# Decode attention, two layers on one core: the scores of heads 2 to 12 move from matmuls to VectorE multiply-and-sums, with their keys laid out by key

## The chip, the core and the metric

The kernel runs on one core of a Trainium2 chip. A core has a matrix engine (TensorE, "PE" in the profile), a vector engine (VectorE, "DVE"), a scalar engine (ScalarE, "ACT"), GpSimd ("POOL") and a queue engine (SyncE, "SP") that here issues nearly all transfers between the chip's memory (HBM) and on-chip memory (SBUF). Matmul results land in a small accumulator memory (PSUM). The metric is the device time of one execution, in microseconds; three timed runs of the kernel before took 1323.81 to 1325.99 us, with a median of 1324.0.

## The reference

The input `x` is two rows (batch 2, one token each) of 448 numbers. Two layers are applied, each an attention over a cache and then a gated feed-forward block, with a layer norm ahead of each and the result added back to `x`. Both layers use the same caches and weights.

```
q = (layernorm(x) @ wq)              # 16 heads of 256
scores = q . k_cache * 256**-0.5     # per head and row: 4096 keys of 256
p = softmax(scores)
o = p . v_cache
x = x + o @ wo
gate = layernorm(x) @ W_gate;  up = layernorm(x) @ W_up     # 448 -> 1792
x = x + (gate * (gate > 0) * up) @ W_down
```

All in float32. One head of one batch row has 4 MB of keys and 4 MB of values, so a layer reads 268 MB of cache, and what the second layer can't find on the chip it reads again.

## The kernel before

**Units.** The work of a layer is cut into 32 units, one for each pair of head and batch row, `u = 0..31`. The first layer takes heads 0 to 15, the second heads 15 to 0, so that the last keys and values of the first layer can stay on the chip (22 chunks of 1 MB, `KEPT`).

**Staging.** SBUF holds an arena of 27 slots of 1 MB: six blocks of four slots and three single ones. Keys and values come as whole 4 MB blocks in one transfer, except near the start of the second layer and the ends of both (`grouped`), where they come by 1 MB. The weights of a head (`wq` and `wo` parts, "h", 896 KB) go to a single slot and leave its last 256 columns free. Feed-forward weights come through the same slots. `pump` issues transfers on SP in one fixed order, as soon as the order of releases in the program frees a slot or a block; each transfer then waits on the chip for the last reader of that place. A unit's order of loads is keys, the next head's weights (every second unit), values.

**A unit.** `query(u)`, once for a head, makes the query of both rows as a column (256 numbers over 128 partitions, two halves) and pads it into `q_pad`. `score(u, c)` is run for four 1 MB chunks: the host has laid the keys out so that a chunk has 128 of a key's 256 numbers down the partitions, and four matmuls of 128x512 per chunk give the scores in PSUM (`rawa` or `rawb`) spread over a few partitions. `score_copy` brings them to `found_s` (VectorE), and `score_turn` turns them by four small matmuls into 128 partitions x 32 columns. `softmax_max` takes the maximum (VectorE, then GpSimd over the partitions), `softmax_exp` the exponentials and their sum (ScalarE, GpSimd). `weigh(u, c)` multiplies them with the values, 16 matmuls of 128x512 a unit into `poa` or `pob`. `softmax_sum`, `out_copy` and `out_add` scale and add the two halves into `row`; `out_turn` and `out_keep` turn that row into a column, and `project` (every second unit) multiplies it with `wo` and adds to `y` in PSUM.

**What sets the order.** The order is written out by hand (`manual_schedule`), and each engine runs its own instructions in that order; semaphores between engines are put in automatically. `scores(u)` interleaves the end of unit `u - 1` (`out_turn`, `out_keep`, `project`) between the chunks of unit `u`; `outputs(u)` follows.

**Layer start.** `absorb` makes the centred input `xT` from `y`. `again` writes the residual back into `y` by two matmuls, so that `project` can add to it. `busy(n, half)` issues n dummy matmuls, whose results nobody reads, between steps in which PE waits.

Of the kernel before, what the change touches and what calls it, by code (L numbers as in the profile page):

```python
# [9 lines left out]
AF = mybir.ActivationFunctionType  # L10
ALU = mybir.AluOpType
# [3 lines left out]
B, D, H, S, DH, F = 2, 448, 16, 4096, 256, 1792  # L15
P = 128
DC = 5
FULL, TAIL = 3, 64
NT = S // P
CT = 8  # L20
UNIT = CT * DH
# [6 lines left out]
SMALL = 13  # L28
ENDS = 4
AHEAD = 4  # L30
EPS = 1e-5
SCALE = DH**-0.5

# [32 lines left out]
def two_layers(  # L66
# [10 lines left out]
    nc = tc.nc  # L77
# [10 lines left out]
    arena = consts.tile([P, (BLOCKS * NC + SINGLES) * UNIT], F32, name="arena")  # L88
# [6 lines left out]
    at_of = {}  # L95
# [16 lines left out]
    def pump():  # L112
        while pending:
            at = None
            for i, ((kind, name, c), n) in enumerate(pending[: AHEAD if pending[0][1] == 1 else 1]):
                if i and kind != "h":
# [20 lines left out]
    def get(*key):  # L137
        at = at_of[key]
        return arena[:, at * UNIT : (at + 1) * UNIT]
# [45 lines left out]
    row = consts.tile([P, 2 * DH], F32, name="row")  # L185
    found_s = consts.tile([P, 2 * DH], F32, name="found_s")
# [23 lines left out]
    eps_t = consts.tile([P, 1], F32, name="eps_t")  # L210
    nc.vector.memset(eps_t, EPS)

# [5 lines left out]
    xT = xr[:, :, :, 0]  # L218
# [3 lines left out]
    raw = [ps_r.tile([P, 2 * DH], F32, name=f"raw{k}") for k in "ab"]  # L222
# [14 lines left out]
    def busy(n, half):  # L237

        for _ in range(n):
            nc.tensor.matmul(  # L240
                po_all[half][:B, :DH], ident[:, :B],
                ident[:, None, :].to_broadcast([P, 2, P]), start=True, stop=True,
            )
# [23 lines left out]
    def again():  # L267

        for half in range(2):
            n = D - DH if half else DH  # L270
            nc.tensor.matmul(
                y[32 * half : 32 * half + B, :n], halves[:, half], yrow[:, :n],
                start=True, stop=False,
            )

    def squares():
        sq = work.tile([P, FULL + 1, B], F32, name="sq")
        nc.vector.tensor_mul(sq, xT[:, : FULL + 1], xT[:, : FULL + 1])
        total = work.tile([P, B], F32, name="total")
        nc.vector.reduce_sum(total, sq.rearrange("p c b -> p b c"), axis=AX.X)  # L280
        return total
# [9 lines left out]
    def attention(order, after):  # L291
# [4 lines left out]
        q_of, oT_of, s_of, mx_of, p_of, r_of, po_of, pT_of = ({} for _ in range(8))  # L296
# [3 lines left out]
        def query(u):  # L300
            h = order[u][0]
            w = get("h", h, 0)
            pq = pq_all
            for j in range(2):
                if j and u == 0:
                    again()
                for c in range(FULL):
                    at = c * DH + j * P
                    nc.tensor.matmul(  # L309
                        pq[:, j, :], w[:, at : at + P], xT[:, c, :], start=(c == 0), stop=False  # L310
                    )
                nc.tensor.matmul(  # L312
                    pq[:, j, :], w[:, FULL * DH : FULL * DH + P], xT[:, FULL + j, :],
                    start=False, stop=True,
                )
            q = q_pad[:, u // 2 % 2]
            nc.vector.tensor_copy(q[..., 1], pq)
            for v in (u, u + 1):
                q_of[v] = q[:, :, order[v][1]]

        def spread(total):

            deviation(total)
            nc.scalar.activation(nsr[:, :1], eps_t, AF.Exp)
            inverse()
            nc.vector.tensor_scalar_mul(sr, rstd, SCALE)
            nc.vector.tensor_scalar_mul(nsr, rstd, -SCALE)
# [42 lines left out]
        def softmax_sum(u):  # L370
            ri = work.tile([P, 1], F32, name="ri")
            nc.vector.reciprocal(ri, r_of[u])
            r_of[u] = work.tile([P, 2], F32, name="ri2")
            nc.vector.tensor_scalar_mul(r_of[u], lead, ri)

        def weigh(u, c):


            vt = get("v", order[u], c)
            if c == 0:  # L380
                po_of[u] = po_all[u % 2]
            for t in range(CT if u == n_u - 1 else 0):
                n = c * CT + t
                nc.tensor.matmul(
                    po_of[u][32 * (t % 4) : 32 * (t % 4) + 1, :DH],
                    p_of[u][:, n : n + 1],
                    vt[:, t * DH : (t + 1) * DH],
                    start=(c == 0 and t < 4),
                    stop=(c == NC - 1 and t >= 4),
                )  # L390
            for t in range(CT // 2 if u < n_u - 1 else 0):
                n = c * CT + 2 * t
                nc.tensor.matmul(  # L393
                    po_of[u][32 * t : 32 * t + 2, :],
                    p_of[u][:, n : n + 2],
                    vt[:, 2 * t * DH : (2 * t + 2) * DH],
                    start=(c == 0),
                    stop=(c == NC - 1),
                )
            if ("v", order[u], c) not in after:  # L400
                release("v", order[u], c)

        def out_copy(u):
            nc.scalar.activation(row[:, :DH], po_of[u][:, :DH], AF.Copy, scale=r_of[u][:, 0:1])  # L404

        def out_add(u):
            if u == n_u - 1:
                return
            nc.vector.scalar_tensor_tensor(  # L409
                row[:, :DH], po_of.pop(u)[:, DH:], r_of[u][:, 1:2], row[:, :DH],  # L410
                op0=ALU.mult, op1=ALU.add,
            )
# [30 lines left out]
        def if_pair(step, u, *more):  # L443
            if 0 <= u < n_u:
                step(u, *more)

        busy(2, 0)
        total = squares()
        query(0)
        busy(1, 0)  # L450

        def scores(u):
            if_pair(score, u, 0)
            if u == 0:
                spread(total)
            if_pair(score, u, 1)
            if_pair(out_turn, u - 1)
            if_pair(out_keep, u - 1)
            if_pair(score, u, 2)
            if_pair(score, u, 3)  # L460
            if_pair(score_copy, u)
            if u == 0:
                busy(1, 0)
            if_pair(project, u - 1)
            if_pair(score_turn, u)
            if u == 0:
                busy(2, 0)
            if_pair(softmax_max, u)
            if_pair(softmax_exp, u)

        def outputs(u):
            for c in range(NC):
                weigh(u, c)
            softmax_sum(u)
            out_copy(u)
            out_add(u)

        for u in range(n_u - 1):
            scores(u)
            if u % 2:  # L480
                query(u + 1)
            if u < n_u - 2:
                outputs(u)
        u = n_u - 1
# [4 lines left out]
        softmax_max(u)  # L489
        softmax_exp(u)  # L490
        outputs(u - 1)
        for c in range(NC):
            weigh(u, c)
# [93 lines left out]
    add(0, ident[:B, :B], row[:B, :D], start=True, stop=True)  # L587
    absorb()
    attention(first, keep)
    ffn(False)  # L590
    absorb()
    attention(second, set())
    ffn(True)
    nc.vector.tensor_add(yrow[: 32 + B], y[: 32 + B], yrow[: 32 + B])
# [8 lines left out]
def _arrays(np, A_x, A_k_cache, A_v_cache, A_wq, A_wo, B_W_gate, B_W_up, B_W_down, **_):  # L603

    rows = FULL * P
    wq = A_wq.reshape(D, H, DH)
    head = [wq[c * P : (c + 1) * P].transpose(1, 0, 2) for c in range(FULL)]
    head.append(wq[rows:].reshape(TAIL, H, 2, P).transpose(1, 2, 0, 3).reshape(H, P, P))
    wo = A_wo.reshape(H, 2, P, D)
    head += [wo[:, 0], wo[:, 1]]  # L610
    full = [w[c * P : (c + 1) * P] for w in (B_W_gate, B_W_up) for c in range(FULL)]
    full.insert(FULL, np.concatenate([B_W_gate[rows:], B_W_up[rows:]]))
    down = B_W_down.reshape(4, D, D)
    chunks = [down[j, m * P : (m + 1) * P] for j in range(4) for m in range(FULL)]
    chunks += [np.concatenate([down[j, rows:], down[j + 1, rows:]]) for j in (0, 2)]
    k = A_k_cache.reshape(B, H, P, 2, E, G, 2, P).transpose(0, 1, 7, 3, 6, 5, 4, 2)
    found = {
        "x": A_x,
        "k_cache": k.reshape(B, H, P, S * 2),
        "v_cache": A_v_cache,  # L620
        "w_head": np.concatenate(head, axis=2),
        "w_in": np.stack(full),
        "w_out": np.concatenate(chunks, axis=1),
    }
    return {n: np.ascontiguousarray(a) for n, a in found.items()}
# [24 lines left out]
```

## Time and profile before

| | us |
|---|---|
| median of three timed runs | 1324.0 |
| the profiled execution | 1326.48 |
| its span, first to last instruction | 1324.7 |
| PE busy | 948.3 |
| DVE busy | 135.6 |
| ACT busy | 91.7 |
| POOL busy | 47.7 |

The profile page gives the share of the span that each engine is busy, then rows of 40 digits, one for each slice of 33 us: a 9 means 90% or more. "PEclk" is the clock that TensorE was granted, in tenths. A row of a group reads: line, engine, operation, output<-inputs, count | busy us, mean ns of one | idle time ahead, and what ended it. In the order of time, a row is start, duration, engine, line and operation, and in brackets the wait ahead of it. A float32 matmul shows as two records.

### The profile page before, as it was taken

How to read it: one execution, taken by the hardware profiler on the slowest of the kernel's cores; microseconds unless marked ns; L12 is line 12 of the kernel's file. 1: busy time of each engine (PE TensorE's matmuls, PEld its weight loads, DVE VectorE, ACT ScalarE, POOL GpSimd, SP SyncE). 2: the span in 40 equal slices, each digit the busy share in tenths (PEclk: the TensorE clock that was granted, in tenths of full speed). 3: DMA queues.
4: the chain of work that ended last, by engine and by line, in shares of the span. 5: the costliest groups of instructions: out<-in, count | busy, mean ns of one | idle time of the engine just before them, and what ended most of it. 6: DMA issues, size and time to landing. Idle time of an engine off the chain costs nothing.

```text
span 1324.7 us, 13815 instructions
## 1 busy us (share of the span) xinstructions
PE 948.3 (72%) x6090; PEld 312.3 (24%) x6090; DVE 135.6 (10%) x458; ACT 91.7 (7%) x279; POOL 47.7 (4%) x134
## 2 busy tenths in 40 slices
PE   5777667666776776767689867666676666766778
PEld 2222122221221221222133322222122221222223
DVE  1101010010000110001001111011010100101001
ACT  1000000000000000000011100000000000000001
POOL 0000000000000000000000000000000000000000
PEclk9767787788667777777798887787777777678679
DMA  9999999999999999999999999999999999999998
GB/s 404 430 430 432 430 426 436 427 434 427 428 432 432 430 430 428 432 433 428 420 378 388 436 428 433 430 428 433 428 432 429 428 432 428 434 431 430 431 421 336
DMA packets 28152, 562.42 MB, mean 425 GB/s; under 512 B 3126, under 2 KB 3260, under 8 KB 10556
## 3 DMA queue, kind: packets, MB, share of 16 engines
q1 hardware_dynamic: 28084, 561.53, 99.3%
q8 instruction: 48, 0.79, 0.2%
q14 instruction: 12, 0.10, 0.0%
q10 hardware_dynamic: 8, 0.01, 0.0%
HBM read 561.52 MB, written 0.00 MB: 424 GB/s over the span
## 4 chain that ended last, share of the span: by engine, by line
PE 57%; another core or an unknown queue 25%; DMA 12%; DVE 3%; issue 2%; ACT 1%; POOL 0%; SPq 0%; POOLq 0%; DVEq 0%; ACTq 0%
PE rawa L333 12%; PE pob L393 11%; PE rawb L333 11%; PE poa L393 10%; PE small L347 4%; DMA arena<-in_k_cache_dram 3%; DMA arena<-in_v_cache_dram 3%; DMA arena<-in_w_in_dram 3%; PE pq L309 3%; PE small L417 3%; DVE found_s L341 2%; DMA arena<-in_w_out_dram 2%; PE pq L312 1%; ACT probs L364 1%
## 5 line engine op out<-in xcount | busy, mean ns | idle before, releaser
L333 PE MATMUL rawa<-arena,q_pad 128*2 128x512 f32 x1024 | 183.4, 848 | 112.1 <-DMA arena<-in_k_cache_dram 112.1
L333 PE MATMUL rawb<-arena,q_pad 128*2 128x512 f32 x1024 | 181.8, 847 | 100.0 <-DMA arena<-in_k_cache_dram 100.0
L393 PE MATMUL poa<-arena,probs 128*2 128x512 f32 x1024 | 168.9, 821 | 58.9 <-DMA arena<-in_v_cache_dram 32.8
L393 PE MATMUL pob<-arena,probs 128*2 128x512 f32 x960 | 164.5, 847 | 44.8 <-DMA arena<-in_v_cache_dram 44.7
L347 PE MATMUL small<-ident,found_s 128*128 128x8 f32 x512 | 69.7, 263 | 34.8 <-DVE found_s L341 34.6
L347 PEld LDWEIGHTS small<-ident,found_s 128*128 128x128 f32 x512 | 63.9, 196 | 96.2 <-DVE found_s L341 96.2
L333 PEld LDWEIGHTS rawa<-arena,q_pad 128*2 128x2 f32 x1024 | 25.1, 96 | 208.8 <-issue 206.0
L393 PEld LDWEIGHTS poa<-arena,probs 128*2 128x2 f32 x1024 | 31.5, 105 | 169.3 <-issue 113.4
L333 PEld LDWEIGHTS rawb<-arena,q_pad 128*2 128x2 f32 x1024 | 24.4, 96 | 198.7 <-DMA arena<-in_k_cache_dram 125.0
L361 ACT ACTIVATE nm<-top,nsr 128x1 f32<-128x1 f32 x64 | 18.8, 294 | 743.2 <-POOL top L356 743.2
L417 PEld LDWEIGHTS small<-ones,row 128*128 128x128 f32 x256 | 44.6, 247 | 92.0 <-issue 85.5
L356 POOL PARTITION_ALL_REDUCE top<-mx x64 | 22.5, 351 | 1167.2 <-DVE mx L354 1150.1
L393 PEld LDWEIGHTS pob<-arena,probs 128*2 128x2 f32 x960 | 27.8, 106 | 154.7 <-issue 154.3
L309 PE MATMUL pq<-xs,arena 128*128 128x2 f32 x384 | 56.3, 263 | 0.0
L309 PEld LDWEIGHTS pq<-xs,arena 128*128 128x128 f32 x384 | 52.6, 208 | 2.8 <-issue 2.4
L417 PE MATMUL small<-ones,row 128*128 128x1 f32 x256 | 50.1, 299 | 0.4 <-ACT row L404 0.4
L426 DVE COPY oT<-small 128x2 f32<-128x2 f32 x64 | 10.2, 160 | 382.1 <-PE small L417 382.1
L409 DVE SCALAR_TENSOR_TENSOR row<-pob,ri,row 128x256 f32<-128x256 f32 x30 | 14.5, 484 | 203.7 <-ACT row L404 203.7
L409 DVE SCALAR_TENSOR_TENSOR row<-poa,ri,row 128x256 f32<-128x256 f32 x32 | 15.5, 484 | 168.9 <-ACT row L404 168.9
L341 DVE COPY found_s<-rawb 128x512 f32<-128x512 f32 x32 | 22.1, 692 | 91.2 <-PE rawb L333 91.2
L404 ACT ACTIVATE row<-pob,ri 128x256 f32<-128x256 f32 x32 | 15.2, 474 | 229.5 <-PE pob L393 221.7
L341 DVE COPY found_s<-rawa 128x512 f32<-128x512 f32 x32 | 22.1, 692 | 71.7 <-PE rawa L333 71.7
(79 smaller groups left out, 316.3 us busy)
## 6 DMA issues: line engine op xcount, KB each, us to landing
arena<-in_k_cache_dram SPq DMA_DIRECT2D x59, 4096.0 KB, 54.6
arena<-in_v_cache_dram SPq DMA_DIRECT2D x58, 4096.0 KB, 55.3
arena<-in_w_head_dram SPq DMA_DIRECT2D x31, 896.0 KB, 54.7
arena<-in_w_in_dram SPq DMA_DIRECT2D x14, 896.0 KB, 16.4
arena<-in_v_cache_dram SPq DMA_DIRECT2D x12, 1024.0 KB, 11.7
arena<-in_k_cache_dram SPq DMA_DIRECT2D x8, 1024.0 KB, 13.3
arena<-in_w_out_dram SPq DMA_DIRECT2D x4, 896.0 KB, 16.8
arena<-in_v_cache_dram SPq DMA_DIRECT2D x4, 512.0 KB, 47.6
```

The source lines that it names most:

```text
L309: nc.tensor.matmul(pq[:, j, :], w[:, at : at + P], xT[:, c, :], start=(c == 0), stop=False)
L312: nc.tensor.matmul(pq[:, j, :], w[:, FULL * DH : FULL * DH + P], xT[:, FULL + j, :], start=False, stop=True,)
L333: nc.tensor.matmul(raw[u % 2][32 * g : 32 * g + 2, :], q_of[u][:, j, 1 - half : 3 - half], kt[:, g, :], start=(c == 0), stop=(c == NC - 1),)
L341: nc.vector.tensor_copy(found_s, raw[u % 2])
L347: nc.tensor.matmul(s[:, :, e, :], found_s[:, e * P : (e + 1) * P], pick, start=True, stop=True,)
L356: nc.gpsimd.partition_all_reduce(mx_of[u], mx, P, RED.max)
L361: nc.scalar.activation(nm, mx_of.pop(u), AF.Copy, scale=nsr[:, b : b + 1])
L364: nc.scalar.activation(p_of[u], s_of.pop(u), AF.Exp, bias=nm, scale=sr[:, b : b + 1], accum_out=rs)
L393: nc.tensor.matmul(po_of[u][32 * t : 32 * t + 2, :], p_of[u][:, n : n + 2], vt[:, 2 * t * DH : (2 * t + 2) * DH], start=(c == 0), stop=(c ...
L404: nc.scalar.activation(row[:, :DH], po_of[u][:, :DH], AF.Copy, scale=r_of[u][:, 0:1])
L409: nc.vector.scalar_tensor_tensor(row[:, :DH], po_of.pop(u)[:, DH:], r_of[u][:, 1:2], row[:, :DH], op0=ALU.mult, op1=ALU.add,)
L417: nc.tensor.matmul(pT_of[u][:, c : c + 1], row[:, c * P : (c + 1) * P], ones, start=True, stop=True,)
```

## The change

For heads 2 to 12 (`BY_KEY`) the host leaves the keys as they are in the cache: partition p holds keys 32p to 32p + 31, each with its 256 numbers in a row. This is also the layout of the values. `query_rows` makes, in place of `query`, the query as a row that stands on all 128 partitions: its stationary operand is one column of `xT` repeated 128 times, and it needs ten matmuls per head (for each batch row three of 128x256 and two of 128x128). ScalarE copies the 128x512 result from PSUM into `found_s`. `score_by_key` then goes through the 32 key columns of a unit: each VectorE instruction multiplies 128x256 of keys with the query row and sums along the row, which gives one column of scores, already at its place (128 x 32, in spare columns of `row`). Its product is written to the 256 free columns of the head's weight slot, the same ones each time. No copy from PSUM and no turning is needed for these units.

The order in these units is another one: the end of unit `u - 1` (`rest`: the scaling and adding, then `out_turn`, `out_keep`, `project`) stands between the chunks of unit `u`. Heads 0, 1, 13, 14 and 15 are computed as before. At a layer's start `again` moves from the middle of the first query to a place ahead of it, and one dummy matmul takes its old place.

```diff
+BY_KEY = range(2, 13)
...
             for j in range(2):
                 if j and u == 0:
-                    again()
+                    busy(1, 0)
...
+        def query_rows(u):
+            h = order[u][0]
+            w = get("h", h, 0)
+            bank = raw[u // 2 % 2]
+            for b in range(B):
+                for c in range(FULL):
+                    nc.tensor.matmul(
+                        bank[:, b * DH : (b + 1) * DH], xT[:, c, b : b + 1].to_broadcast([P, P]),
+                        w[:, c * DH : (c + 1) * DH], start=(c == 0), stop=(c == FULL - 1),
+                    )
+                    for j in range(2 if c == 0 else 0):
+                        nc.tensor.matmul(
+                            bank[:, b * DH + j * P : b * DH + (j + 1) * P],
+                            xT[:, FULL + j, b : b + 1].to_broadcast([P, P]),
+                            w[:, FULL * DH : FULL * DH + P], start=False, stop=False,
+                        )
+            nc.scalar.activation(found_s, bank, AF.Copy)
+
+        def score_by_key(u, c):
+            h, b = order[u]
+            kt = get("k", order[u], c)
+            at = at_of["h", h, 0] * UNIT + UNIT - DH
+            s_of[u] = row[:, DH + NT * (u % 2) : DH + NT * (u % 2 + 1)]
+            for t in range(CT):
+                n = c * CT + t
+                nc.vector.tensor_tensor_reduce(
+                    out=arena[:, at : at + DH], in0=kt[:, t * DH : (t + 1) * DH],
+                    in1=found_s[:, b * DH : (b + 1) * DH], scale=1.0, scalar=0.0,
+                    op0=ALU.mult, op1=ALU.add, accum_out=s_of[u][:, n : n + 1],
+                )
+            if ("k", order[u], c) not in after:
+                release("k", order[u], c)
...
-        busy(2, 0)
+        again()
+        busy(1, 0)
         total = squares()
         query(0)
         busy(1, 0)
...
+        def next_query(u):
+            if u % 2:
+                (query_rows if by_key(u + 1) else query)(u + 1)
+
+        def rest(u):
+            softmax_sum(u)
+            out_copy(u)
+            out_add(u)
+
+        def scores_by_key(u):
+            score_by_key(u, 0)
+            score_by_key(u, 1)
+            rest(u - 1)
+            out_turn(u - 1)
+            score_by_key(u, 2)
+            out_keep(u - 1)
+            score_by_key(u, 3)
+            project(u - 1)
+            next_query(u)
+            softmax_max(u)
+            softmax_exp(u)
...
         def outputs(u):
             for c in range(NC):
                 weigh(u, c)
-            softmax_sum(u)
-            out_copy(u)
-            out_add(u)
+            if not by_key(u + 1):
+                rest(u)
...
+    k = k.reshape(B, H, P, S * 2)
+    for h in BY_KEY:
+        k[:, h] = A_k_cache[:, h].reshape(B, P, S * 2)
```

**VectorE, in the steady part of the first layer, before** (one unit; `found_s` is the copy of the scores, `mx` the maximum, `q_pad` the next head's query, `row` the added halves, `oT` the turned output; what an instruction waits for stands in brackets):

```order
L341 COPY found_s<-rawb 128x512 [waits PE_49]
L354 TENSOR_REDUCE mx<-small 128x1 [waits PE_49]
L317 COPY q_pad<-pq 128x4 [waits PE_49]
L372 RECIPROCAL ri<-total 128x1 [waits Pool_49]
L374 TENSOR_SCALAR ri_289<-lead,ri 128x2 [waits DVE_49]
L409 SCALAR_TENSOR_TENSOR row<-pob,ri_289,row 128x256 [waits Activation_49]
L426 COPY oT<-small 128x2 [waits PE_49]
```

**VectorE, in unit 4 (head 2), now**, around the middle of the unit's keys. "ISA" with 128x256 is the multiply-and-sum; "ISA row 128x1" reads its sum out:

```order
L347 ISA arena,row<-arena,found_s 128x256 [waits DVE_49]
L347 ISA row 128x1
L406 RECIPROCAL ri<-total 128x1 [waits Pool_49]
L408 TENSOR_SCALAR ri_444<-lead,ri 128x2 [waits DVE_49]
L443 SCALAR_TENSOR_TENSOR row<-pob,ri_444,row 128x256 [waits Activation_49]
L347 ISA arena,row<-arena,found_s 128x256
L347 ISA row 128x1
L347 ISA arena,row<-arena,found_s 128x256 [waits DVE_49]
```

The copies of scores and query are gone, 32 pairs a unit are new, and the end of the unit before stands between them. Each pair behind the first waits for the one ahead of it, on VectorE's own semaphore.

**PE at the start of a layer, before** (`pq` is the query, `y<-found_s,halves` the re-entry of the residual, `poa<-ident` the dummies):

```order
L261 MATMUL pq<-nlead,sums 128x10
L240 MATMUL poa<-ident 2x256 x2
L309 MATMUL pq<-xs,arena 128x2 x3
L312 MATMUL pq<-xs,arena 128x2
L271 MATMUL y<-found_s,halves 2x256
L271 MATMUL y<-found_s,halves 2x192
L309 MATMUL pq<-xs,arena 128x2 x3
L312 MATMUL pq<-xs,arena 128x2
L240 MATMUL poa<-ident 2x256
```

**The same place now:**

```order
L262 MATMUL pq<-nlead,sums 128x10
L272 MATMUL y<-found_s,halves 2x256
L272 MATMUL y<-found_s,halves 2x192
L241 MATMUL poa<-ident 2x256
L310 MATMUL pq<-xs,arena 128x2 x3
L313 MATMUL pq<-xs,arena 128x2
L241 MATMUL poa<-ident 2x256
L310 MATMUL pq<-xs,arena 128x2 x3
L313 MATMUL pq<-xs,arena 128x2
L241 MATMUL poa<-ident 2x256
```

The two re-entry matmuls and one dummy have changed places. On SP the transfers, their sizes and their order are what they were; the wait for the last reader of keys is now one for VectorE in the units by key.

More of the change, by code (lines that the diff above doesn't have):

```diff
@@ L450, in attention, with by_key @@
         busy(1, 0)
+        def by_key(u):
+            return order[u][0] in BY_KEY
+        def next_query(u):
[17 more added lines that the diff above has]
+            softmax_exp(u)
         def scores(u):
+            if by_key(u):
+                return scores_by_key(u)
             if_pair(score, u, 0)
@@ L469, in scores @@
             if_pair(softmax_exp, u)
+            next_query(u)
         def outputs(u):
@@ L473, in outputs @@
                 weigh(u, c)
-            softmax_sum(u)
-            out_copy(u)
-            out_add(u)
+            if not by_key(u + 1):
+                rest(u)
         for u in range(n_u - 1):
             scores(u)
-            if u % 2:
-                query(u + 1)
             if u < n_u - 2:
@@ L616, in _arrays @@
     k = A_k_cache.reshape(B, H, P, 2, E, G, 2, P).transpose(0, 1, 7, 3, 6, 5, 4, 2)
+    k = k.reshape(B, H, P, S * 2)
+    for h in BY_KEY:
+        k[:, h] = A_k_cache[:, h].reshape(B, P, S * 2)
     found = {
         "x": A_x,
-        "k_cache": k.reshape(B, H, P, S * 2),
+        "k_cache": k,
         "v_cache": A_v_cache,
```

## The prediction

> **What bounds the kernel now.** I read the page first (busy shares, the DMA rows, the issues), then the busy time by stage, then the order of time inside one steady unit.
>
> ```profile
> PE 948.3 (72%) x6090; PEld 312.3 (24%) x6090; DVE 135.6 (10%) x458; ACT 91.7 (7%) x279; POOL 47.7 (4%) x134
> DMA  9999999999999999999999999999999999999998
> GB/s 404 430 430 432 430 426 436 427 434 427 428 432 432 430 430 428 432 433 428 420 378 388 436 428 433 430 428 433 428 432 429 428 432 428 434 431 430 431 421 336
> q1 hardware_dynamic: 28084, 561.53, 99.3%
> arena<-in_k_cache_dram SPq DMA_DIRECT2D x59, 4096.0 KB, 54.6
> arena<-in_v_cache_dram SPq DMA_DIRECT2D x58, 4096.0 KB, 55.3
> ```
>
> PE is busy for 72%, but the DMA engines are busy for 99.3%, at about 430 GB/s in nearly every slice. A block of 4 MB lands 54.6 us after its issue; at 430 GB/s it takes 4.19 MB / 430 = 9.75 us of that, so more than four other blocks are queued ahead of it. The dips are the feed-forward stage between the layers (slices of 378 and 388) and the last slice.
>
> ```profile
> 300.00:500.00 200.00, 142.50 (x860) 43.69 (x852) 20.02 (x65) 12.38 (x40) 7.33 (x20) 0.73 1.01 431
> 387.44:428.49 41.05, 29.99 (x177) 9.02 (x178) 4.00 (x13) 2.48 (x8) 1.47 (x4) 0.71 1.00 429
> 660.00:680.00 20.00, 16.58 (x171) 6.31 (x163) 2.10 (x11) 3.51 (x7) 0.00 (x0) 1.00 0.94 368
> 680.00:700.00 20.00, 18.76 (x143) 9.05 (x144) 1.82 (x8) 1.52 (x4) 0.00 (x0) 0.83 0.92 355
> 720.00:740.00 20.00, 17.28 (x140) 5.07 (x132) 3.20 (x9) 1.71 (x5) 0.73 (x2) 0.90 1.04 439
> ```
>
> Columns: stretch, its length, busy PE, PE weight load, DVE, ACT, POOL, granted clock, DMA share, GB/s. In the steady stage the DMA share is 1.00 or more while PE idles for more than a quarter; only the feed-forward stretches are below.
>
> ```profile
> 387.44 3.59 PE rawa L333 x16
> 406.78 3.49 PE L333 MATMUL rawb<-arena,q_pad 128*2 128x512 f32 x16 [2.45 <-DMA arena<-in_k_cache_dram]
> 412.70 0.33 SPq L133 DMA_DIRECT2D arena<-in_k_cache_dram  x1
> 418.78 6.03 PE L393 MATMUL pob<-arena,probs 128*2 128x512 f32 x32 [2.49 <-DMA arena<-in_v_cache_dram]
> 424.88 0.33 SPq L133 DMA_DIRECT2D arena<-in_v_cache_dram  x1
> 428.49 3.60 PE L333 MATMUL rawa<-arena,q_pad 128*2 128x512 f32 x16 [3.68 <-DMA arena<-in_k_cache_dram]
> ```
>
> Scores and weighing each begin when their block lands, and each hands its block back at once: keys land at 406.8, and the transfer into their place is issued at 412.7, 5.9 us later. Two units take 428.49 - 387.44 = 41.05 us, so a unit's budget is 20.5 us. Any engine that stays under it is hidden behind the transfers.
>
> **The change, part by part.** *Scores on VectorE.* Forty-four units (eleven heads, two batch rows, two layers) each get 32 multiply-and-sums over 128x256. In the order each is a pair, the main instruction and one that reads the sum out, and the next main one waits on VectorE's own semaphore, because all write the same scratch columns. The trace of before has no such pair. Its nearest rows:
>
> ```profile
> L550 DVE TENSOR_TENSOR row<-rawb,row 128x448 f32<-128x448 f32 x2 | 1.2, 624 | 7.2 <-PE rawb L517 7.2
> L278 DVE TENSOR_TENSOR sq<-xs 128x8 f32<-128x8 f32 x4 | 0.7, 172 | 0.1
> L409 DVE SCALAR_TENSOR_TENSOR row<-poa,ri,row 128x256 f32<-128x256 f32 x32 | 15.5, 484 | 168.9 <-ACT row L404 168.9
> L364 ACT ACTIVATION_READ_ACCUMULATOR probs<-small,nm,sr 128x1 f32 x64 | 12.2, 191 | 0.0
> L341 DVE COPY found_s<-rawb 128x512 f32<-128x512 f32 x32 | 22.1, 692 | 91.2 <-PE rawb L333 91.2
> L333 PE MATMUL rawa<-arena,q_pad 128*2 128x512 f32 x1024 | 183.4, 848 | 112.1 <-DMA arena<-in_k_cache_dram 112.1
> 18.35 0.17 DVE L265 TENSOR_TENSOR xs<-pq,mask 128x10 f32<-128x10 f32 x1 [3.82 <-PE pq L261]
> 18.56 0.17 DVE L278 TENSOR_TENSOR sq<-xs 128x8 f32<-128x8 f32 x1
> 33.48 0.38 ACT L364 ACTIVATE probs<-small,nm,sr 128x32 f32<-128x32 f32 x1
> 33.76 0.19 ACT L364 ACTIVATION_READ_ACCUMULATOR probs<-small,nm,sr 128x1 f32 x1
> ```
>
> Main instruction: the two multiplies give (624 - 172) / 440 = 1.03 ns an element, so 172 + 248 x 1.03 = 427 ns at 256. The other bound is 484, a multiply-add of that very size, which also takes a per-partition factor; the new one has constants, so I take 427. Reading the sum: ScalarE's read lasts 191 ns but starts 0.10 before its main instruction ends, so it adds 0.09; bounds 0 (hidden) and 0.191. The wait: L278 starts 0.04 after the end of L265, on whose result it depends; bounds 0 and 0.04. Together 0.427 + 0.09 + 0.04 = 0.557 us a key tile, between 0.427 and 0.484 + 0.191 + 0.04 = 0.715. Thirty-two make 17.8 us (13.7 to 22.9).
>
> What stays on VectorE: 4.00 us of the two-unit row, less two 0.692 copies out of PSUM and about 0.16 for the query's copy, is 1.2 a unit; five waits of 0.04 add 0.2. New is a wait for the next head's query: ScalarE writes `found_s` only after the last tile that reads the old one, and the next unit's tiles queue behind it. That is a 128x512 copy, 0.69 by L341 (another engine's; 0 if the keys are not there yet), once in two units: 0.35. **Unit: 17.8 + 1.2 + 0.2 + 0.35 = 19.6 us against 20.5** (15.5 to 24.7). By this sum VectorE stays just hidden; uncovered, the surplus over 20.5 counts 22 times in each layer.
>
> The surplus would not show at once. Keys would be held about 20.5 us instead of 5.9, 14.6 more; of the 54.6 us between issue and landing, less one transfer, 54.6 - 9.75 - 14.6 = 30 us remain before the DMA engines run dry. A surplus of e costs a layer 22e - 30: nothing up to e = 1.4, a unit of 21.9 us, or (21.9 - 1.75) / 32 = 0.63 us a tile.
>
> A rule that speaks against the change: the Trainium skill, page "Vector Engine (DVE) Microarchitecture Reference", section "Points that are easy to get wrong", says that an accumulating two-source form with two non-bf16 SBUF sources runs at half throughput. No row of before tests it: the one multiply quoted with both sources in SBUF, L278, has 8 elements and its 172 ns are nearly all fixed. By the rule the sum would be the second price of rival B; by the rows, the one above.
>
> *Freed and added on PE.* Score matmuls go: 183.4 us over 32 units, 5.7 a unit, and the four that turn them. The row-wise query issues ten matmuls (20 records) per head; at no more than the 848 ns of a record twice as wide that is under 17 us per two units. The 41.05 - 29.99 = 11 idle and the 11.5 freed cover it. PE's lower use gives nothing while transfers set the pace.
>
> *Transfers.* Sizes, blocks and SP's order are the same; the keys' new layout is made on the host. Each release is later, not reordered.
>
> *The re-entry's two matmuls.* At the second layer's start PE is on the path, since the first key chunks are handed back only after the first scores:
>
> ```profile
> 691.17 1.02 PE L240 MATMUL poa<-ident 128*2 128x256 f32 x4
> 691.28 0.17 DVE L265 TENSOR_TENSOR xs<-pq,mask 128x10 f32<-128x10 f32 x1 [7.33 <-PE pq L261]
> 692.13 0.83 PE L309 MATMUL pq<-xs,arena 128*128 128x2 f32 x6
> 693.11 0.82 PE L271 MATMUL y<-found_s,halves 128*2 128x256 f32 x4
> 693.86 0.37 PE L309 MATMUL pq<-xs,arena 128*128 128x2 f32 x1
> ```
>
> The two dummies take 691.17 to 692.13, 0.48 each; the re-entry takes 693.11 to 693.86, 0.75. Before: 0.96 + 0.98 (first half of the query) + 0.75 = 2.69 to the second half. After: 0.75 + 0.48 + 0.98 + 0.48 = 2.69. The query's input is ready at 691.45, before PE gets there either way. Zero; if it went wrong, at most one dummy, 0.5.
>
> **Sum:** 0 + 0 + 0. The profiled execution took 1326.5 (span 1324.7); the three timed runs have a median of 1324.0, so no change means 1324.0.
>
> **Rivals.** *B, VectorE becomes the bound*, from 0.63 us a tile on. At the upper bound, 0.715, e = 24.7 - 20.5 = 4.2: 22 x 4.2 - 30 = 62 a layer, 124 in all, 1448. If two SBUF sources run at half rate, the main instruction takes 172 + 2 x 255 = 682, the tile 0.81, the unit 27.7, and 2 x (22 x 7.2 - 30) = 257: 1581. For it: the margin is under 1 us, and the pair is unknown. Against: every VectorE row here follows about one element in 1.03 ns.
>
> *C, the lag reaches the ends.* With tiles at 0.59 to 0.63 the transfers stay fed, but the keys' lag (14.6 + 22e) has only heads 1 and 0, four units, to be made up before the end.
>
> ```profile
> 717.09 5.24 PE pob L393 x32
> 742.95 3.54 PE pob L393 x32
> ```
>
> PE catches up at (742.95 - 717.09) / 2 = 12.9 us a unit, 7.6 under the budget, 30 in four units. At e = 1.2 the lag is 41: 11 us late, about 1335.
>
> *D, the transfers run faster* once PE no longer streams keys. Forty-four units are 903 us; at the best slice, 436 for 430 GB/s, they would save 903 x 6 / 436 = 12: 1312. Against it: the stretch at 720 us has PE at 17.28 of 20 and 439 GB/s, the most PE and the most bytes.
>
> That the change does not do what it says is excluded: the order has 1,408 such pairs.
>
> **How the numbers follow.** No change (A) 0.62, B 0.20 (0.12 near its first price or below, 0.08 for half rate), C 0.06, D 0.12. Within 0.2%, 2.6 us, is about what a measurement can tell from no change: same 0.62, slower 0.26, faster 0.12. The time is A's, 1324.0; its own range is 1322 to 1327. For 8 in 10 the range takes in C, half of D (down to 1317) and the shallow part of B, up to 0.67 us a tile: unit 23.2, e = 2.7, 2 x (59 - 30) = 58, so 1385, with some room 1390. That is 0.62 + 0.06 + 0.06 + 0.08 = 0.82.
>
> **What the new profile would show.** Right: the DMA row stays at 99%, VectorE at about 17 us more in each of 44 units (some 900 us in all), still idle behind key landings; issue to landing of key blocks falls by some 12 us to near 42. B wrong or right: the tile's cadence against 0.63, and key blocks issued late with gaps in the GB/s row from the first third of a layer on. C: dips only at the ends. D: steady slices above 436. The forecast is wrong if tiles run beyond 0.63, or if the layer's start at 691 us changes by more than 1 us.

## The result, and the profile after

The changed kernel takes 1340.3 us (median of four runs, 1339.8 to 1342.4) where the kernel before takes 1324.0 beside it: 1.0119 times as long, with a 95% interval of 1.0107 to 1.0132. It is slower by about 16 us. The forecast was no change.

The page of the kernel after, with the engines, the bytes of 40 slices, the DMA queues and the two large issues:

```profile
PE 710.5 (53%) x4418; PEld 297.0 (22%) x4418; DVE 696.2 (52%) x3208; ACT 106.3 (8%) x301; POOL 47.8 (4%) x134
GB/s 399 433 433 432 427 425 438 428 429 429 431 430 430 430 431 431 428 432 431 410 290 372 438 426 431 432 431 428 429 432 433 426 430 434 428 430 431 433 419 254
q1 hardware_dynamic: 28084, 561.53, 98.2%
q8 instruction: 35, 0.57, 0.2%
q14 instruction: 33, 0.27, 0.1%
arena<-in_k_cache_dram SPq DMA_DIRECT2D x59, 4096.0 KB, 47.4
arena<-in_v_cache_dram SPq DMA_DIRECT2D x58, 4096.0 KB, 51.0
```

VectorE did not become the bound: it is busy for 52%. The slices are at 430 as before, except at two places: the dip between the layers fell from 378 and 388 to 290 and 372 (with 410 ahead of it for 420), and the last slice from 336 to 254. One small row has grown: the instruction queue q14 carries 33 packets (0.27 MB, so 8 KB each). Before, the rows of the two instruction queues were:

```profile
q8 instruction: 48, 0.79, 0.2%
q14 instruction: 12, 0.10, 0.0%
```

The busy time by stretch (columns as in the prediction) of the kernel after:

```profile
300.00:500.00 200.00, 85.94 (x477) 37.55 (x479) 137.76 (x647) 15.25 (x44) 7.35 (x20) 0.70 1.00 431
640.00:660.00 20.00, 12.59 (x84) 3.45 (x84) 2.10 (x5) 0.88 (x4) 0.73 (x2) 0.83 0.99 418
660.00:680.00 20.00, 15.94 (x150) 6.44 (x150) 2.21 (x12) 2.19 (x7) 0.76 (x2) 0.91 0.55 221
680.00:700.00 20.00, 16.56 (x154) 6.70 (x150) 1.30 (x5) 2.56 (x5) 0.00 (x0) 1.00 0.99 389
700.00:720.00 20.00, 18.92 (x125) 7.24 (x125) 2.93 (x12) 2.99 (x7) 0.74 (x2) 0.83 0.84 336
1320.00:1340.00 20.00, 15.28 (x144) 5.24 (x136) 1.72 (x6) 2.47 (x4) 0.00 (x0) 1.00 0.40 162
```

The kernel before, for the two stretches that the prediction doesn't show:

```profile
640.00:660.00 20.00, 14.31 (x100) 4.32 (x96) 2.06 (x6) 1.52 (x6) 1.49 (x4) 0.74 0.98 415
700.00:720.00 20.00, 18.11 (x142) 7.04 (x138) 3.53 (x12) 2.70 (x9) 1.47 (x4) 0.93 1.00 415
```

The steady part moves 431 GB/s, exactly as before. From 640 to 720 us, which holds the dip of both kernels, the DMA engines stand idle for (0.01 + 0.45 + 0.01 + 0.16) x 20 = 12.6 us on average, where it was (0.02 + 0.06 + 0.08 + 0.00) x 20 = 3.2: 9.4 us more. When the first layer's transfers end can be read from SP's queue, where the feed-forward weights are issued into the slots that come free; here of the kernel after, then of before:

```profile
644.28 37.18 SPq L134 DMA_DIRECT2D arena<-in_w_in_dram  x7
```

```profile
635.09 37.55 SPq L133 DMA_DIRECT2D arena<-in_w_in_dram  x7
```

Of the 15.7 us between the two spans (1340.4 and 1324.7), 9.2 are lost by the end of the first layer, about the idle time that was added there. Yet no slice of that layer shows a loss. So the loss shows only where the queue of transfers runs empty, and need not arise there.

**Where it hides.** The trace also keeps the completion marks of the transfers. Each large transfer leaves 16, as many as the core has DMA engines; I read one mark as one engine's share being done. The block can be used when the last mark is there. For the transfers around a given time, the last mark stands behind the middle of the 16 by (us):

```
around (us)           202   304   405   500   601   660 |  700   998  1100  1205  1300
before                1.1   1.6   1.8   0.6   2.0   2.1 |  1.3   2.4   2.3   3.2   2.7
after                 2.9   5.6   8.5  10.5  12.1  11.2 |  1.3   4.4   7.3   9.3  10.3
after, next-to-last   0.5   0.3   0.6   1.8   1.5       (first layer)
```

In the kernel after, one of the 16 shares comes later and later, by 12 us at the end of the first layer, while the 15th comes 0.3 to 1.8 us behind the middle as before. The lag falls back to 1.3 us in the feed-forward stage, when the transfers stop and the late engine can catch up, and grows again in the second layer. Listed transfer by transfer it grows in steps of mostly 0.9 to 1.0 us. In the first layer, from 160 us on, each of these steps has a fetch of 8 KB of instructions by q14 between the late mark of one transfer and the late mark of the next. So the theory, T1: **VectorE got some 2,750 more instructions (3,208 for 458); they have to be fetched from memory; the fetches are served by one of the DMA engines, which are all full; that engine falls behind by about 1 us for each fetch, and every block lands when its slowest engine is done.** The rival, R1: VectorE hands the keys back later than PE did, and the lag has to be paid at a layer's end (the prediction's rival C).

### The profile page after: what moved, and what is told of

Read it like the earlier page. It is cut to its first block, busy times and chain, and to the rows that moved or that the text cites. A ratio compares the mean times of both kernels' runs of the same rounds, so it can differ in the third digit from the quotient of the medians.

```text
span 1340.4 us, 13247 instructions
## 1 busy us (share of the span) xinstructions
PE 710.5 (53%) x4418; PEld 297.0 (22%) x4418; DVE 696.2 (52%) x3208; ACT 106.3 (8%) x301; POOL 47.8 (4%) x134
## 4 chain that ended last, share of the span: by engine, by line
DMA 67%; DVE 18%; PE 6%; another core or an unknown queue 5%; issue 2%; ACT 1%; SPq 0%; POOL 0%; ACTq 0%; DVEq 0%; POOLq 0%
DMA arena<-in_k_cache_dram 58%; DVE arena L347 16%; DMA arena<-in_v_cache_dram 4%; DMA arena<-in_w_in_dram 3%; DMA arena<-in_w_out_dram 2%; PE pob L427 1%; PE rawa L367 1%; PE poa L427 1%; PE rawb L367 1%; DVE row L347 1%; DVE row L443 1%; ACT row L438 1%; PE pq L310 0%; PE small L381 0%
## 5 line engine op out<-in xcount | busy, mean ns | idle before, releaser
L347 DVE CUSTOM_DVE_ANT_0 arena<-arena,found_s 128x256 f32<-128x256 f32 x1408 | 597.0, 424 | 256.4 <-DMA arena<-in_k_cache_dram 212.2
L427 PE MATMUL pob<-arena,probs 128*2 128x512 f32 x960 | 127.9, 681 | 54.1 <-ACT probs L398 50.7
L347 DVE DVE_READ_ACCUMULATOR2_ANT row<- 128x1 f32 x1408 | 114.2, 81 | 0.0
L367 PE MATMUL rawb<-arena,q_pad 128*2 128x512 f32 x320 | 52.4, 790 | 27.1 <-DMA arena<-in_k_cache_dram 27.1
L250 PE MATMUL y<-arena,oT 128*2 128x192 f32 (+1 forms) x256 | 28.8, 492 | 58.6 <-DVE oT L460 58.6
L367 PE MATMUL rawa<-arena,q_pad 128*2 128x512 f32 x320 | 46.5, 694 | 14.4 <-DMA arena<-in_k_cache_dram 14.4
L328 PE MATMUL rawa<-arena,xs 128*128 128x256 f32 x132 | 53.1, 545 | 0.0
L328 PE MATMUL rawb<-arena,xs 128*128 128x256 f32 x132 | 51.4, 529 | 0.0
L328 PEld LDWEIGHTS rawa<-arena,xs 128*128 128x128 f32 x132 | 34.5, 289 | 4.5
L328 PEld LDWEIGHTS rawb<-arena,xs 128*128 128x128 f32 x132 | 33.2, 278 | 4.2
## 6 DMA issues: line engine op xcount, KB each, us to landing
arena<-in_k_cache_dram SPq DMA_DIRECT2D x59, 4096.0 KB, 47.4
arena<-in_w_in_dram SPq DMA_DIRECT2D x14, 896.0 KB, 16.3
arena<-in_v_cache_dram SPq DMA_DIRECT2D x4, 512.0 KB, 47.4
```

The lines of the kernel that those rows point to most:

```text
L250: nc.tensor.matmul(bank[at : at + B, : w_h.shape[1]], stat, w_h, **flags)
L328: nc.tensor.matmul(bank[:, b * DH : (b + 1) * DH], xT[:, c, b : b + 1].to_broadcast([P, P]), w[:, c * DH : (c + 1) * DH], start=(c == 0), ...
L347: nc.vector.tensor_tensor_reduce(out=arena[:, at : at + DH], in0=kt[:, t * DH : (t + 1) * DH], in1=found_s[:, b * DH : (b + 1) * DH], scal ...
L367: nc.tensor.matmul(raw[u % 2][32 * g : 32 * g + 2, :], q_of[u][:, j, 1 - half : 3 - half], kt[:, g, :], start=(c == 0), stop=(c == NC - 1),)
L427: nc.tensor.matmul(po_of[u][32 * t : 32 * t + 2, :], p_of[u][:, n : n + 2], vt[:, 2 * t * DH : (2 * t + 2) * DH], start=(c == 0), stop=(c ...
```

## The experiments

Those that only add instructions write or multiply values that nobody reads; they leave all else of the kernel as it is. All ratios are to the kernel before, timed beside it on the same chip.

### The instructions without the change

```diff
+        def small(u, c):
+            if 2 <= order[u][0] < 13:
+                for n in range(16 * c, 16 * c + 16):
+                    nc.vector.memset(row[:, D + n : D + n + 1], 0.0)
```

It is called once behind each chunk of scores; the last call stands behind `score_copy`.

> The kernel before, with scores still on PE, and 64 writes of 128x1 zeros into unused columns of `row` on VectorE in each unit of heads 2 to 12 (16 behind each chunk of scores; the result isn't touched). They add 2,816 instructions to VectorE, as many as the multiply-and-sums and their reads, but only some 64 x 0.06 = 4 us of work a unit, far under the 20.5 us budget, and no key is handed back later. Theory T1 (the fetching of VectorE's instructions slows one of the 16 DMA engines, and a block lands when its slowest engine is done): the loss of the change comes back without the change, about 1340 us (1336 to 1343); q14 has some 34 packets, and the last of the 16 engines is about 10 us behind the middle one by 600 us. Rival R1 (keys are released late by VectorE): no change, 1322.5 to 1325.5.

Measured: 1340.5 us, 1.0116 (1.0102 to 1.0130). The page, and the stretch between the layers:

```profile
PE 957.9 (72%) x6090; PEld 319.2 (24%) x6090; DVE 173.7 (13%) x3274; ACT 91.8 (7%) x279; POOL 48.0 (4%) x134
GB/s 400 434 432 426 431 428 432 431 431 429 428 431 430 431 431 428 427 434 428 412 308 410 427 431 433 427 430 432 430 425 434 429 429 432 427 431 433 429 418 256
q14 instruction: 34, 0.28, 0.1%
```

```profile
660.00:680.00 20.00, 15.95 (x154) 6.30 (x157) 2.10 (x11) 2.19 (x7) 0.76 (x2) 0.91 0.60 235
```

Scores are on PE, VectorE is busy for 13%, and nearly the whole loss of the change is there, 15.4 us of 16.3, with similar dips (308 and 256 for 290 and 254) and 34 packets for 33. The last of the 16 marks is 10.6 us behind the middle by 600 us. R1 can't explain this: no key is released by VectorE here.

### The change with few instructions

```diff
-            for t in range(CT):
-                n = c * CT + t
-                nc.vector.tensor_tensor_reduce(
-                    ...
-                )
+            keys = kt.rearrange("p (t d) -> p t d", d=DH)
+            nc.vector.tensor_mul(
+                keys, keys, found_s[:, None, b * DH : (b + 1) * DH].to_broadcast([P, CT, DH])
+            )
+            nc.vector.reduce_sum(s_of[u][:, c * CT : (c + 1) * CT], keys, axis=AX.X)
```

> The changed kernel, but each 1 MB chunk of keys is multiplied by the query row in one VectorE instruction of 128x2048 (in place) and summed in a second one, so 8 instructions a unit instead of 64. VectorE's time a chunk is no shorter (at about 1.03 ns an element twice, 2 x 2.1 = 4.2 us against 8 x 0.466 = 3.7), so keys are handed back later, not sooner. T1: the loss goes with the instructions: 1322 to 1327, q14 near its 12 packets of before, the last engine some 3 us behind at most. R1: no better than 1340, rather worse, about 1342 to 1350.

Measured: 1323.5 us, 0.9990 (0.9981 to 0.9999). The loss is gone, although VectorE has more to do than in the change; the page, and the order of time around one unit on VectorE:

```profile
PE 688.9 (52%) x4418; PEld 256.0 (19%) x4418; DVE 884.5 (67%) x744; ACT 106.6 (8%) x301; POOL 118.8 (9%) x134
GB/s 405 425 434 429 429 429 435 428 436 426 428 437 428 431 431 427 435 427 431 422 393 397 433 433 433 425 434 430 428 433 432 429 430 430 432 430 431 431 423 345
q14 instruction: 15, 0.12, 0.0%
L346 DVE TENSOR_TENSOR arena<-arena,found_s 128x2048 f32<-128x2048 f32 x176 | 401.9, 2283 | 52.0 <-DMA arena<-in_k_cache_dram 40.8
L349 DVE TENSOR_REDUCE row<-arena 128x8 f32<-128x2048 f32 x176 | 402.4, 2286 | 6.1
arena<-in_k_cache_dram SPq DMA_DIRECT2D x59, 4096.0 KB, 42.5
```

```profile
402.68 0.15 DVE L458 COPY oT<-small 128x2 f32<-128x2 f32 x1
402.74 2.28 DVE L346 TENSOR_TENSOR arena<-arena,found_s 128x2048 f32<-128x2048 f32 x1
...
422.46 0.15 DVE L458 COPY oT<-small 128x2 f32<-128x2 f32 x1
422.53 2.28 DVE L346 TENSOR_TENSOR arena<-arena,found_s 128x2048 f32<-128x2048 f32 x1
```

A unit takes VectorE 422.53 - 402.74 = 19.8 us, with hardly a gap, against 20.5 of a unit's transfers, and keys are held longer than in the change (issue to landing is 42.5, not 47.4). This is nearly the unit that the prediction expected of the change (19.6), and it costs nothing. It is the best version measured, but 0.1% is less than a measurement of this kernel can tell from no change.

### Twice the instructions

The `small` writes of above, added to the changed kernel.

> The changed kernel with the same 64 writes of 128x1 zeros a unit added on VectorE (the result isn't touched), so twice the added instructions and about 4 us more of VectorE's time in each unit, which stays under the 20.5 us budget or just at it (15 + 1.5 + 4 = 20.5). T1: the loss about doubles, to 1352 to 1360, and the late engine's lag too. R1 (release time of the keys): 4 us more once, so at most 1345.

Measured: 1361.5 us, 1.0284 (1.0268 to 1.0300), 36.5 us above before: 2.2 times the change's 16.3, and 1.5 us above the range that was expected.

```profile
GB/s 398 437 429 429 430 432 430 431 429 428 429 429 432 432 429 428 431 426 433 291 286 407 429 428 430 433 431 430 428 429 431 430 430 429 430 430 431 430 317 231
q14 instruction: 55, 0.45, 0.1%
```

The steady slices are still at 430. The dips are wider now (291, 286 and 317, 231), and the lag of the last mark is 22.8 us by the first layer's end.

### Half the heads

```diff
-BY_KEY = range(2, 13)
+BY_KEY = range(2, 8)
```

> The changed kernel with heads 2 to 7 by key instead of 2 to 12: 12 of a layer's units instead of 22. T1: the loss goes with the number of instructions, 12/22 of 16 us, about 1333 (1330 to 1336), half in each layer, although ten units by matmul follow in the first layer, because the late engine is not waited for by the others. R1 in its last form (keys released late, to be made up behind the last unit by key): nothing in the first layer, where ten units by matmul follow, and at most 2 us more than the full change in the second, where heads 1 and 0 follow as before; in all about half of the change's loss too, but all of it behind the second layer.

Measured: 1331.8 us, 1.0054 (1.0039 to 1.0069), 6.9 us. More telling is where it sits. The end of the first layer on SP's queue:

```profile
639.88 37.27 SPq L134 DMA_DIRECT2D arena<-in_w_in_dram  x7
```

The first layer ends 639.88 - 635.09 = 4.8 us late, although its last eight heads are all computed by matmul and had 16 units (not ten, as the expectation counts them) to make up for late keys. The fetches of q14, and the lag of the last mark by the time of the transfer, from the trace's records (us):

```
fetches   215, 255, 294, 331, 333, 338, none until 535
lag       212: 3.3   221: 4.3   243: 4.3   253: 5.2   284: 5.2   294: 6.2   323: 6.1   335: 7.1   405: 7.0   448: 6.9
```

Each fetch adds 0.9 to 1.0 us; when the fetches end, the lag stays. A late engine isn't waited for by the others while four blocks are queued, so it keeps its lag until the queue runs empty. (Of 333 and 338 no step is seen; which instructions they brought I can't tell.)

### The other engines' instructions

The same `small` writes on GpSimd, then as copies on ScalarE, then every second one on GpSimd and the rest on VectorE; and 16 small matmuls a unit on PE, which the trace counts as 64 matmul and weight-load records:

```diff
-                    nc.vector.memset(row[:, D + n : D + n + 1], 0.0)
+                    nc.gpsimd.memset(row[:, D + n : D + n + 1], 0.0)
...
+                    nc.scalar.activation(row[:, D + n : D + n + 1], lead[:, 0:1], AF.Copy)
...
+                    (nc.gpsimd if n % 2 else nc.vector).memset(row[:, D + n : D + n + 1], 0.0)
...
+                for n in range(4):
+                    nc.tensor.matmul(
+                        bank_q[:B, 60 + n : 61 + n], ident[:, :B], ident[:, :1], start=True, stop=True,
+                    )
```

> The kernel before with the same 64 writes a unit put on GpSimd instead of VectorE. If the cost belongs to the fetching of any engine's instructions (T1, wide form), the time is again near 1340 and another instruction queue shows some 20 packets more; if it belongs to VectorE's stream alone (T1, narrow form), the time stays at 1322.5 to 1326. Rival R1 says no change as well, but it has already lost to the VectorE run; this run separates the two forms of T1.

> The kernel before with 64 copies of 128x1 a unit on ScalarE (at about 0.2 us each 13 us of work a unit, beside 20.5; 16 of them stand ahead of each unit's exponentials, so the exponentials may come up to 3 us later, which the slack of a unit covers). T1, wide form: near 1340, with some 20 packets more on ScalarE's instruction queue. Narrow form: 1322.5 to 1327.

> The kernel before with the 64 small writes a unit shared out, every second one on GpSimd, so 11 more fetches for each of the two streams. If both streams are served by the same DMA engine, the lags add: half of 15.4 and half of 5.5 us, about 1335.5 (1333.5 to 1337.5). If each has its own, only the later one counts: half of 15.4, about 1332.5 (1330 to 1333.5).

> The kernel before with 16 matmuls of two rows by one column a unit of heads 2 to 12 added on PE (4 behind each chunk of scores, into unused columns of `pq`'s accumulator, which nobody reads). Each is two matmul and two weight-load records, so again 2,816 instructions, and at some 0.3 us each 5 us of a unit in which PE idles for 5.5. If PE's instruction fetches (q8, 48 of 16 KB before) cost what VectorE's do, 11 more of them fall on one DMA engine and the time is 1335 to 1340; if they are spread over the engines, as the steady lag of before under 3.2 us suggests, 1323 to 1327.

Measured: GpSimd 1330.4 us, 1.0040 (1.0025 to 1.0054); ScalarE 1333.1, 1.0061 (1.0046 to 1.0076); shared out 1330.1, 1.0040 (1.0025 to 1.0055); PE 1328.2, 1.0026 (1.0016 to 1.0036). The instruction queues, in that order:

```profile
q14 instruction: 33, 0.27, 0.0%
```

```profile
q14 instruction: 34, 0.28, 0.1%
```

```profile
q14 instruction: 33, 0.27, 0.1%
```

```profile
q8 instruction: 59, 0.97, 0.3%
q14 instruction: 12, 0.10, 0.0%
```

Neither the wide nor the narrow form of T1 came out as put. The instructions of all three engines arrive by q14, and the same number of fetches costs 15.4 us for VectorE, but 8.2 for ScalarE and 5.5 for GpSimd. The marks show a part of the reason: at a fetch, the late mark falls back by 0.9 to 1.0 us with VectorE's writes, but by 0.6 to 0.8 with GpSimd's or ScalarE's.

Sharing them out cost 5.7 us, far below the 9.2 to 13.2 of one DMA engine for both streams and just at the lower end of the 5.7 to 9.2 expected of two. The marks of this run decide it. Two of the 16 fall back, in turn, each at fetches of its own (first layer, from 200 to 510 us; the lag behind the middle, in us):

```
fetch at                230    259    297    340    367    406    440    489    501
the last mark grew by   0.97    -     0.97    -     0.91    -     1.02    -     0.95
the 15th mark by         -     0.67    -     0.65    -     0.66    -     0.65    -
```

(At one more fetch, at 330, neither moves.) By their size the upper steps are VectorE's and the lower ones GpSimd's: each stream delays a DMA engine of its own, and a block waits only for the later of the two. PE's eleven fetches of 16 KB more cost 3.9 us (2.1 to 4.8), more than the "spread" case allowed and far less than on one engine; the last mark is 3.0 us behind by 600 us, for 2.0 before.

### The re-entry alone

```diff
@@ query
                 if j and u == 0:
-                    again()
+                    busy(1, 0)
@@ start of a layer
-        busy(2, 0)
+        again()
+        busy(1, 0)
```

> The kernel before with only the other part of the change: the residual's re-entry ahead of the layer's first query, one dummy matmul in its old place. The prediction's step says 0: 1323.5 to 1324.5. A rival that puts the loss at the layer's start says up to +1 us a layer.

Measured: 1324.8 us, 1.0001 (0.9992 to 1.0010). This part of the change costs nothing.

### All runs by one number

The lag of the last mark (median over the last blocks of each layer, 560 to 655 and 1240 to 1300 us), the sum of what it has over the kernel before, and the time that was lost (the median less that of the kernel before timed beside it, 1324 to 1325 us), in us:

```
                              layer 1  layer 2   sum over before   time over before
before                          2.0      2.8            -                  -
the re-entry alone              1.7      3.1          -0.1               -0.3
change, few instructions        2.4      1.8          -0.6               -1.6
PE, 16 small matmuls            3.0      3.5           1.7                3.9
shared out                      4.7      3.5           3.4                5.7
GpSimd, 64 writes               6.1      4.3           5.6                5.5
half the heads                  6.6      4.5           6.3                6.9
ScalarE, 64 copies              6.8      5.4           7.4                8.2
VectorE, 64 writes             10.6      8.6          14.4               15.4
the change                     12.1     10.3          17.6               16.3
the change + 64 writes         22.8     20.7          38.7               36.5
```

The time lost follows the two lags within 2.3 us in every row, whatever the kernel computes and on whichever engine. Of R1 nothing is seen: the few-instruction version holds keys longest and loses nothing. A few us of it are not excluded, because that version, like the change, also has 13 fewer fetches for PE (35 for 48). By the price of PE's run, 3.9 us for eleven, these would be worth 4.6 us (an estimate), and 1.6 were gained.

## Why the prediction was wrong

**The step that failed: "Transfers. Sizes, blocks and SP's order are the same".** This was true of the transfers that the program issues, and I took it to mean that they land as before. It left out a transfer that no line of the program issues: the instructions themselves. The page before had the row (q14, 12 packets), the order showed 1,408 pairs more for VectorE, beside 458 instructions on its page (3,208 in the new one), and the whole argument rested on DMA engines that are full for 99.3%. Put together they ask for the price of some 21 more packets on full engines. By the page's sum it looks like nothing: 21 packets of 8 KB are 0.17 MB of 561. By the slowest engine, at the 0.95 us a fetch that the marks show, it is 21 x 0.95 = 20 us by estimate, if all 21 fall on one engine and it isn't ahead of the others at first; 16.3 were measured. The Trainium skill, page "Runtime: NRT & Kernel Launch", section "Instruction fetch mechanics", says that crossing a block of instructions costs a bump of a DMA tail and is mostly hidden; here, with full DMA engines, the runs disagree: 22 fetches more cost 15.4 us with nothing else added but small writes.

**The forecast's own case, A, had the right picture of VectorE.** The few-instruction version, by other instructions, is that case: a unit of 19.8 us against 20.5, no loss, and DMA at 430. The budget and the idle engine's price of nothing held.

**The terms for the pair.** The groups and the order of time of the kernel after:

```profile
L347 DVE CUSTOM_DVE_ANT_0 arena<-arena,found_s 128x256 f32<-128x256 f32 x1408 | 597.0, 424 | 256.4 <-DMA arena<-in_k_cache_dram 212.2
L347 DVE DVE_READ_ACCUMULATOR2_ANT row<- 128x1 f32 x1408 | 114.2, 81 | 0.0
```

```profile
413.56 0.42 DVE L347 CUSTOM_DVE_ANT_0 arena<-arena,found_s 128x256 f32<-128x256 f32 x1 [3.85 <-DMA arena<-in_k_cache_dram]
413.91 0.08 DVE L347 DVE_READ_ACCUMULATOR2_ANT row<- 128x1 f32 x1
414.03 0.42 DVE L347 CUSTOM_DVE_ANT_0 arena<-arena,found_s 128x256 f32<-128x256 f32 x1
```

The multiply-and-sum takes 424 ns (predicted 427). The read of the sum, put at 0.09 us beyond the main instruction, starts 0.07 before its end (413.91 against 413.98) and adds 0.01; the wait is 0.04 as put. From 413.56 to 414.03 a pair takes 0.47 us, not 0.557, so 32 take 15 us, and VectorE idles 3.85 us for the next keys. The total is 696 us, not "some 900", and issue to landing 47.4, not "near 42", for that reason.

**Rival B** (VectorE the bound) fell: its point was 0.63 us a tile. Its second price, from the rule that an accumulating two-source form with both sources in SBUF runs at half throughput (the Trainium skill, "Vector Engine (DVE) Microarchitecture Reference", "Points that are easy to get wrong"), does not hold for this instruction: that would have been 682 ns, and the trace has 424. Whether the page's form is the one that runs here, the trace doesn't say.

**Rival C** named 1335 us and dips only at the ends, and both are close, by luck. Its mechanism is not what happened: it needed tiles of 0.59 to 0.63 us and late keys. The same dips appear with PE releasing the keys early, and vanish with VectorE releasing them later still. **Rival D** (transfers faster without PE's stream) fell: 431 GB/s in the steady part in both. (The argument against it called the stretch at 720 us the one with the most PE; 680 to 700 has more, 18.76 of 20 us, at 355 GB/s.) One sum is off by a little: 58 us on 1324.0 are 1382, not 1385.

**The re-entry** was put at 0, and alone it measured 1.0001 times the kernel before. In the chain of waits of the kernel after, the same piece:

```profile
700.22 0.52 PE y L272 x3
701.18 0.76 PE pq L310 x6
702.16 0.92 PE poa L241 x2
703.08 1.37 PE pq L310 x6
```

From the re-entry to the second half it takes 703.08 - 700.22 = 2.86 us, for 2.69 worked out.

**The signs of failure that I named** were tiles beyond 0.63 us, which did not come, and a layer's start at 691 us that changes by more than 1 us. The start's own steps did not change by that much, but it came 9 us later (700.22 for 691.17), and nothing in the prediction says what that would mean. The one sign that did show, dips only at the ends, I had tied to one cause.

## What to carry to other kernels

Where the DMA engines are the bound, count the instructions as transfers too: here every 130 instructions added to VectorE (2,750 over 21 packets) were 8 KB more on one DMA engine, and 22 such fetches cost 15.4 us, about 0.7 us each, so two wide instructions beat sixteen narrow ones even though they keep VectorE busy for longer. Total bytes and the mean DMA share of the steady part don't show it, since a block lands with its slowest engine; look at the packets of the instruction queues, and at the stretch where the transfers run out. A loss that appears at the end of a stage need not arise there.

## What was not expected of the hardware

- One fetch of 8 KB for VectorE puts one DMA engine back by 0.9 to 1.0 us, although its packet is recorded with 0.3 us. What the rest is, the runs don't show.
- Equal numbers of fetches by the same queue cost 15.4 us for VectorE, 8.2 for ScalarE and 5.5 for GpSimd. A fetch puts the late mark back by less there, 0.6 to 0.8 us for 0.9 to 1.0. What is left, and the difference between ScalarE and GpSimd, may be that their DMA engines start ahead of the middle (the first mark of their runs is some 3 us ahead by the end of the first layer); this stays open. The marks carry no engine's name: that a stream is served by one engine is inferred, from the single late mark of one stream and the two of the run that shares the writes out.
- A late DMA engine hardly catches up while the queue is full: in the run with half the heads the lag was 7.1 us at 335 and still 6.7 at 519, with one fetch at the start of that stretch and none behind it.
- PE's fetches, 16 KB each on another queue, are 48 before and 35 after the change and leave no engine far behind. In the kernel before they seem to go round the engines: with one fetch ahead of each, the four latest marks are 0.4, 0.5, 0.6 and 1.7 us behind the middle at 510, then 0.5, 0.6, 1.7 and 2.0 at 541, 0.6, 1.7, 2.0 and 2.0 at 570, and 1.7, 2.0, 2.0 and 2.0 at 602. Of the 3.9 us that eleven more of them cost, 1.7 are seen in the marks. Fetches that go round also move the middle along, which a lag behind the middle can't show; at about 1.05 us a recorded packet that is 11 x 1.05 / 16 = 0.7 us, an estimate. For the rest no run here has a place.
